# Attention and two gated MLPs on one core: k'v of two heads as two 64x64 products, tokens in five even chunks

## The chip, the core and the metric

The kernel runs on one core of one Trainium2 chip. The metric is the device time of one execution in microseconds (us). A core has a matrix engine (PE, with its weight loads written PEld), a vector engine (DVE), a scalar engine (ACT), GpSimd (POOL) and a queue engine (SP) that issues all DMAs of this kernel; one core's DMAs run on 16 DMA engines.

## What is computed

Three layers in a row, in float32, on 8 batches of 576 tokens with 8 heads of 64 features:

```python
def _attn_ref(q, k, v, g_norm):
    kv = np.einsum('bhsd,bhse->bhde', k, v)          # 64 x 64 for each batch and head
    out = np.einsum('bhsd,bhde->bhse', q, kv)
    rms = np.sqrt(np.mean(out * out, axis=-1, keepdims=True) + 1e-06)
    return out / rms * g_norm

def _moe_ref(x, w_gate, w_val, w_out):               # 4608 x 512, width 1536
    return (1 / (1 + np.exp(-(x @ w_gate))) * (x @ w_val)) @ w_out

def _moe2_ref(x, w_in, w_out):                       # width 2048
    h = x @ w_in
    g = np.where(h >= 1, h, np.where(h <= -1, 0.0, (h + 1) ** 2 / 4))
    return g @ w_out
```

The change is in the first line, the sum over 576 tokens that gives `kv`.

## The kernel before

Tokens go through in nine blocks of 512 (`T`). Two heads make a pair: 128 features, one chunk of x. A large product is three float32r products of halves of its operands (`mm3`, L77 to L79), each of a 128x128 weight tile with 512 columns. The order of instructions on every engine is the order in which the code is written (`tc.manual_schedule()`).

The sum k'v of one batch b and pair p is made by `kv_sum(b, p)` (L109 to L115), 32 times in all. Its tokens lie on the partitions. 576 tokens are four chunks of 128 (`NSC`) and a rest of 64 (`SR`); each chunk is one float32 product of 128 columns of k with 128 columns of v (L113), the rest another with 64 rows (L114), all into one 128x128 tile of PSUM, `kvps`. Only the two 64x64 blocks on its diagonal are k'v of the two heads; `kv_blocks` (L117) copies these into the block-diagonal tile `kvbd`, and `attn_out` (L130) multiplies q with it into `X`. A float32 product is two records of the matrix engine in the trace, so one sum is eight records of L113 and two of L114.

What a sum reads is loaded by SP. For batches 0 and 1, `load_kv_early` (L84) issues a load of k (L88), one of v (L89), 256 KB each on 128 partitions, and one of the rest (L90, 64 partitions, 64 KB); a load of q (256 KB) follows each. SP's order at the start is the four pairs of batch 0 (k, v, rest, q each), `eye`, `spread_f`, two 512 KB loads of weights (L267), the four pairs of batch 1, four more loads of weights. For batches 2 to 7, `load_kv` (L93) loads k and v of a pair in one DMA of 512 KB (L95, tile `kvraw`) and the rest in another (L97). A `kvraw` tile lies in the same ring of four buffers as the raw weights. 

The stages: sums of batch 0 and 1, their norms (`SSt` L171, `rt` L190, `R` L203) and the first gate and value products (`h`, from L77), in one written order up to 52 us; then two blocks through all gate and value products while the weights are decoded from float64 (56 to 193 us; the sums of batch 2 stand here, two at a time, without other work between them); then the down products of these two blocks (193 to 258 us), where blocks of g come back from DRAM (`load_g` L397, DMA at L399, `gload`) and the sums of batch 3 stand; then blocks 2 to 8 one after another, with the sums of batches 4 to 7 beside them, one at a time; from 900 us on the second MLP.

Of the kernel before, what the change touches and what calls it, by code (L numbers as in the profile page):

```python
# [7 lines left out]
F32 = mybir.dt.float32  # L8
# [5 lines left out]
B, H, S, D = 8, 8, 576, 64  # L14
NT, DM, FF1, FF2 = B * S, H * D, 1536, 2048
P = 128
T = 512                 # tokens of a block
NB = NT // T
NP = H // 2             # pairs of heads: one chunk of 128 features each
KC = DM // P  # L20
TC = T // P
F1, F2 = FF1 // P, FF2 // P
NSC = S // P            # whole chunks of 128 tokens of a batch; half a chunk remains
SR = S - NSC * P
NKV = 3                 # batches whose k'v is held
EPS = 1e-6


# [1 line left out]
def attn_gated_mlp_kernel(ctx: ExitStack, tc: tile.TileContext, a: dict, out: bass.AP):  # L30
# [30 lines left out]
        nc.vector.tensor_copy(out=o, in_=i)  # L61

    def split(src, hi, lo):
        """A float32 tile as the exact sum of two tiles of twelve bits each."""
        act_copy(hi, src)
        nc.vector.tensor_tensor(out=lo, in0=src, in1=hi.bitcast(F32), op=ALU.subtract)  # L66
        return hi, lo
# [5 lines left out]
        return tp.tile([P, T], F32, name=name, tag=tag, **kw)  # L73

    def mm3(ps, w, x, first, last, wsl=slice(None)):
        """ps += w.T @ x of float32 operands, as three products of their halves."""
        nc.tensor.matmul(ps, w[0][:, wsl], x[0], start=first, stop=False)  # L77
        nc.tensor.matmul(ps, w[0][:, wsl], x[1], start=False, stop=False)  # L78
        nc.tensor.matmul(ps, w[1][:, wsl], x[0], start=False, stop=last)  # L79

# [1 line left out]
    kvraw, qraw, xnext, state, xs = {}, {}, {}, {}, {}  # L82

    def load_kv_early(b, p):  # L84
        k, v, r = (wp.tile([P, T], F32, name="kv_early", tag="w") for _ in range(3))
        k, v = (x.rearrange("p (c n) -> p c n", c=NSC) for x in (k, v))
        r = r[0:SR, 0:2 * P].rearrange("p (i n) -> p i n", i=2)
        nc.sync.dma_start(out=k, in_=a["kv_main"][b, p][:, 0])  # L88
        nc.sync.dma_start(out=v, in_=a["kv_main"][b, p][:, 1])  # L89
        nc.sync.dma_start(out=r, in_=a["kv_rest"][b, p])  # L90
        kvraw[b, p] = k, v, r

    def load_kv(b, p):  # L93
        t = tp.tile([P, 2, NSC, P], F32, name="kvraw", tag="raw", bufs=4)
        nc.sync.dma_start(out=t, in_=a["kv_main"][b, p])  # L95
        r = tp.tile([SR, 2, P], F32, name="kvrest", tag="rest", bufs=2)
        nc.sync.dma_start(out=r, in_=a["kv_rest"][b, p])  # L97
        kvraw[b, p] = t[:, 0], t[:, 1], r
# [9 lines left out]

    def kv_sum(b, p):  # L109
        k, v, r = kvraw.pop((b, p))  # L110
        ps = at_p.tile([P, P], F32, name="kvps", tag="at")
        for c in range(NSC):
            nc.tensor.matmul(ps, k[:, c, :], v[:, c, :], start=c == 0, stop=False)  # L113
        nc.tensor.matmul(ps, r[:, 0, :], r[:, 1, :], start=False, stop=True)  # L114
        return ps  # L115

    def kv_blocks(b, p, ps, copy):  # L117
        for e in range(2):
            s = slice(e * D, (e + 1) * D)
            copy(kvbd[b % NKV][s, p, s], ps[s, s])  # L120

    def segments(j):
        t = j * T
# [4 lines left out]
            t = e  # L128

    def attn_out(j, p, sqtag="sq", x=None):  # L130
        """q (k'v) of a pair of heads, its product with g_norm and its square."""
        q = qraw.pop((j, p))
        X = at_p.tile([P, T], F32, name="X", tag="at")
        for b, t0, t1 in segments(j):
            nc.tensor.matmul(X[:, t0:t1], kvbd[b % NKV][:, p, :], q[:, t0:t1], start=True, stop=True)  # L135
        if x is None:
            x = xnext[p] = xp.tile([P, T], F32, name="xn", tag=f"xn{p}")
        nc.scalar.activation(out=x, in_=X, func=AF.Copy, scale=gn)
        sq = temp("sq", sqtag)
        nc.scalar.activation(out=sq, in_=X, func=AF.Square)  # L140
        return sq
# [16 lines left out]
        nc.vector.reciprocal(out=r, in_=r)  # L158

    def newton(m, r, t):  # L160
        """r * t is 1 / sqrt(m) to float32's accuracy."""
        nc.scalar.activation(out=t, in_=r, func=AF.Square)
        nc.vector.tensor_tensor(out=t, in0=t, in1=m, op=ALU.mult)
        nc.scalar.activation(out=t, in_=t, func=AF.Copy, scale=-0.5, bias=1.5)

    # while other work is short: the norms of all heads together, tokens on the partitions
    def early_squares(j, p, sq):
        if p == 0:
            state[j] = acc_p.tile([P, TC, H], F32, name="SSt", tag="acc0")
# [33 lines left out]
            nc.tensor.matmul(R, spread[:, p, :], state[j][i], start=i == 0, stop=i == 1)  # L203
        nc.vector.tensor_tensor(out=xnext[p], in0=xnext[p], in1=R, op=ALU.mult)

    # the same with heads on the partitions
    def middle_squares(j, p):
        sq = state.pop((j, p))
        if p == 0:
# [13 lines left out]
        nc.vector.tensor_tensor(out=r, in0=r, in1=t, op=ALU.mult)  # L223
        state[j] = split(r, *(tp.tile([H, T], F32R, name="rt", tag=g) for g in ("sq", "sql")))

    # beside other work: each pair of heads on its own, sums on every partition of its head
    def late_norm(j, p):
        hi, lo = state.pop((j, p))
        SS = at_p.tile([P, T], F32, name="SS", tag="at")
# [11 lines left out]
        nc.vector.tensor_tensor(out=x, in0=x, in1=t, op=ALU.mult)  # L241

    def late_piece(j, n):
        """Step n of 9 that make x of a block, beside other work."""
        p = n // 2
        if n % 2 == 0:
            if p:
                late_scale(j, p - 1)
            if p < NP:
                attn_high(j, p)  # L250
                attn_low(j, p)
                if p + 2 < NP:
                    load_q(j, p + 2)
        else:
            late_norm(j, p)
# [3 lines left out]
            hi, lo = tiles[c] if tiles else (half_tile(xp, f"xh{c}", f"xh{c}"), half_tile(xp, f"xl{c}", f"xl{c}"))  # L259
            xs[c] = split(xnext.pop(c), hi, lo)  # L260

# [1 line left out]
    raws, wgv, wo, wos = {}, {}, {}, {}  # L263

    def load_raw(key, src):
# [2 lines left out]
        raws[key] = raw  # L268

    def decode_steps(keys, outs, place=None):  # L270
        """The float32 nearest to each float64, from its two words."""
        rs = [raws.pop(k) for k in keys]
        low, high = [r[:, :, 0] for r in rs], [r[:, :, 1] for r in rs]
        n = range(len(rs))
        t = [temp("dt", "dt", bufs=2) for _ in n]
        u = [temp("du", "du", bufs=2) for _ in n]
        tu, uu = ([x.bitcast(U32) for x in y] for y in (t, u))
        for i in n:
            nc.scalar.activation(out=t[i], in_=high[i].bitcast(F32), func=AF.Abs, scale=2.0 ** -112)  # L279
        yield  # L280
        for i in n:
            nc.vector.tensor_scalar(out=uu[i], in0=tu[i], scalar1=3, scalar2=None, op0=ALU.logical_shift_left)
            yield
        for i in n:
            nc.vector.tensor_scalar(out=tu[i], in0=tu[i], scalar1=3, scalar2=0x7F800000, op0=ALU.logical_shift_left, op1=ALU.bitwise_and)
            yield
        for i in n:
            nc.vector.scalar_tensor_tensor(out=t[i], in0=low[i], scalar=2.0 ** -52, in1=t[i], op0=ALU.mult, op1=ALU.mult)
            yield
        for i in n:  # L290
            nc.vector.tensor_tensor(out=u[i], in0=u[i], in1=t[i], op=ALU.add)
            yield
        outs += [place(k) for k in keys] if place else t
        ou = [x.bitcast(U32) for x in outs]
        for i in n:
            nc.vector.scalar_tensor_tensor(out=ou[i], in0=high[i], scalar=0x80000000, in1=uu[i], op0=ALU.bitwise_and, op1=ALU.bitwise_or)
            yield

    def run(steps, n=None):
        """The next n steps, or all that remain."""  # L300
        while n != 0 and next(steps, steps) is not steps:
            n = n and n - 1

# [21 lines left out]
                wgv[f, i] = split(t, half_tile(wp, "w", "w"), half_tile(wp, "w", "w"))  # L325

    def decode_gv_steps(f, *parts):
        """The halves (gate and value) of a chunk of weights, step by step."""
        outs = []
        yield from decode_steps([("gv", f, i) for i in parts], outs)  # L330
        for i, t in zip(parts, outs):
            decoded[f, i] = t
# [6 lines left out]
            load_raw(("wo", f), a["w_o1"][f])  # L339

    def decode_wo(*fs):
        """Kept as they are, or left in DRAM while their place is taken."""
        aside = {4: "gl", 5: "gh"}

        def place(key):
            f = key[1]
            if f in aside:
                return gp.tile([P, T], F32, name="wof", tag=aside[f])
            return wp.tile([P, T], F32, name="wo", tag="w")

        ts = []
        yield from decode_steps([("wo", f) for f in fs], ts, place)
        for f, t in zip(fs, ts):
            if f in aside:
                nc.sync.dma_start(out=wod[f], in_=t)
            else:
                wo[f] = t
# [9 lines left out]
    def split_wo(src, f):  # L367
        wos[f] = split(src[f], half_tile(tp, "woh", "woh", bufs=2), half_tile(tp, "wol", "wol", bufs=2))

# [1 line left out]
    gs, gf, acc = {}, {}, {}  # L371

    def gv_sum(f, i, xs, bank=None, between=None):
# [41 lines left out]
            (act_copy if c % 2 else dve_copy)(t, acc[c])  # L415
            nc.sync.dma_start(out=dst(c), in_=t)

# [1 line left out]
    w2, wo2, g2 = {}, {}, {}  # L419

    def load_w2(f):
# [15 lines left out]
        return h  # L437

    def act2(j, f, h):
        # t = clip((h + 1) / 2, 0, 1); the activation is t * max(h, t)  # L440
        t = temp("t2", "sig")
        nc.scalar.activation(out=t, in_=h, func=AF.Relu, bias=half, scale=0.5)  # L442
        g = temp("g2", "gf")
# [17 lines left out]
    def rows(j):  # L461
        return lambda c: out[j * T + c * P:j * T + (c + 1) * P, :]

# [1 line left out]
    todo = [(f, i) for f in range(F2) for i in range(2)]  # L465
    with tc.manual_schedule():
        for p in range(NP):
# [32 lines left out]
        nc.scalar.activation(out=half, in_=half, func=AF.Sqrt)  # L500
        nc.gpsimd.memset(half, 0.5)

        # two blocks through the first products at once, while the weights come in
        def early_attention(j, xs):
            sq = {}
            for n in range(NP + 2):
# [259 lines left out]
```

## Time and profile before

| what | value |
|---|---|
| device time, median of 3 runs | 1824.23 us (1816.62 to 1824.81) |
| profiled execution: span from first to last instruction | 1813.3 us |
| PE busy | 1801.8 us, 99% of the span |
| PE weight loads busy | 1468.4 us, 81% |
| DVE busy | 1056.5 us, 58% |
| ACT busy | 753.6 us, 42% |
| records of the k'v sums on PE | 256 of L113, 64 of L114 |

Of the profiled execution the page gives the span; the device times are longer by what lies ahead of the first instruction and behind the last, 10.9 us at the median. Matmul records overlap each other, so PE's busy share says that it seldom waits, not that each record is as short as it can be: for the time that one takes, read the distance from one start to the next.

### The profile page before, as it was taken

What the parts mean: (1) busy time and instruction counts of PE and PEld (TensorE: products, weight loads), DVE (VectorE), ACT (ScalarE), POOL (GpSimd) and SP (SyncE); (2) the same over time, 40 slices, a digit from 0 to 9 for tenths busy, and PEclk for the clock granted to TensorE, in tenths of its full rate; (3) what the DMA queues carried; (4) which work ended last, traced back from release to release, by engine and by line L of the source; (5) the groups of instructions that cost most, each with busy time, mean ns of one, the idle gap of its engine ahead of it and who ended that gap; (6) DMA issues with size and microseconds to landing.
All of it is one profiled execution on the core that took longest, in us unless ns stands there. A gap on an engine that the chain in (4) does not pass through costs nothing.

```text
span 1813.3 us, 20577 instructions
## 1 busy us (share of the span) xinstructions
PE 1801.8 (99%) x7952; PEld 1468.4 (81%) x7952; DVE 1056.5 (58%) x1621; ACT 753.6 (42%) x1233; POOL 1.8 (0%) x9
## 2 busy tenths in 40 slices
PE   8999999999999999999999999999999999999999
PEld 6787788888888888887888888888888888888887
DVE  3788745756667575775633555454545555555554
ACT  4354344545454454554532434343433333333333
POOL 0000000000000000000000000000000000000000
PEclk9999999999999999999999999999999999999999
DMA  7554623131322322112022201010101010101000
GB/s 222 179 170 161 209 95 104 49 119 67 100 73 66 108 76 78 59 59 76 7 70 82 98 30 47 1 47 1 47 1 47 0 47 0 47 1 47 1 24 24
DMA packets 55954, 124.10 MB, mean 68 GB/s; under 512 B 6568, under 2 KB 8744, under 8 KB 55856
## 3 DMA queue, kind: packets, MB, share of 16 engines
q1 hardware_dynamic: 55856, 122.79, 20.4%
q8 instruction: 62, 1.02, 0.2%
q14 instruction: 36, 0.29, 0.1%
HBM read 88.69 MB, written 34.08 MB: 68 GB/s over the span
## 4 chain that ended last, share of the span: by engine, by line
PE 98%; DVE 1%; DMA 0%; issue 0%; ACT 0%; SPq 0%; DVEq 0%; ACTq 0%
PE h L77 18%; PE h L78 18%; PE h L79 18%; PE acc L77 13%; PE acc L79 13%; PE acc L78 13%; PE X L135 2%; PE kvps L113 2%; PE kvps L114 1%; PE SSt L171 0%; PE R L203 0%; PE SS L230 0%; PE SS L231 0%; DMA gload<-gd 0%; DMA kv_early<-in_kv_main 0%
## 5 line engine op out<-in xcount | busy, mean ns | idle before, releaser
L77 PE MATMUL h<-xh,w 128*128 128x512 f32 x1344 | 527.3, 392 | 0.0
L78 PE MATMUL h<-xl,w 128*128 128x512 f32 x1344 | 525.5, 391 | 0.0
L79 PE MATMUL h<-xh,w 128*128 128x512 f32 x1344 | 524.7, 390 | 0.2 <-DVE w L66 0.2
L77 PEld LDWEIGHTS h<-xh,w 128*128 128x128 f32 x1344 | 252.8, 188 | 56.4 <-ACT dt L279 0.4
L79 PEld LDWEIGHTS h<-xh,w 128*128 128x128 f32 x1344 | 252.7, 188 | 55.3 <-DVE w L66 0.6
L78 PEld LDWEIGHTS h<-xl,w 128*128 128x128 f32 x1344 | 252.7, 188 | 54.0
L444 DVE SCALAR_TENSOR_TENSOR g<-t,h 128x512 f32<-128x512 f32 x144 | 98.9, 687 | 249.9 <-ACT t L442 248.8
L442 ACT ACTIVATE t<-h,half 128x512 f32<-128x512 f32 x144 | 99.2, 689 | 261.0 <-PE h L79 261.0
L388 DVE TENSOR_TENSOR gf<-sig,h 128x512 f32<-128x512 f32 x108 | 74.0, 685 | 194.1 <-PE h L79 102.9
L66 DVE TENSOR_TENSOR wol<-wo,woh 128x512 fp32r<-128x512 f32 x252 | 172.5, 685 | 15.4 <-ACT woh L58 15.4
L77 PE MATMUL acc<-gh,woh 128*128 128x512 f32 x432 | 177.2, 410 | 0.0
L79 PE MATMUL acc<-gh,wol 128*128 128x512 f32 x432 | 171.2, 396 | 0.1
L78 PE MATMUL acc<-gl,woh 128*128 128x512 f32 x432 | 171.0, 396 | 0.0
L58 ACT ACTIVATE woh<-wo 128x512 fp32r<-128x512 f32 x252 | 155.5, 617 | 14.2 <-PE acc L79 13.5
L77 PE MATMUL acc<-woh,gh 128*128 128x512 f32 x384 | 150.5, 392 | 0.0
L79 PE MATMUL acc<-woh,gl 128*128 128x512 f32 x384 | 150.2, 391 | 0.0
L78 PE MATMUL acc<-wol,gh 128*128 128x512 f32 x384 | 149.4, 389 | 0.0
L58 ACT ACTIVATE gh<-gf 128x512 fp32r<-128x512 f32 x84 | 53.0, 631 | 212.8 <-DVE gf L388 212.8
L58 ACT ACTIVATE gh<-g 128x512 fp32r<-128x512 f32 x96 | 60.7, 632 | 143.4 <-DVE g L445 143.4
L386 ACT ACTIVATE sig<-h 128x512 f32<-128x512 f32 x108 | 64.6, 598 | 115.4 <-PE h L79 107.6
L66 DVE TENSOR_TENSOR gl<-g,gh 128x512 fp32r<-128x512 f32 x96 | 66.5, 693 | 67.0 <-ACT gh L58 67.0
L445 DVE SCALAR_TENSOR_TENSOR g<-t,g 128x512 f32<-128x512 f32 x144 | 99.5, 691 | 5.0
(127 smaller groups left out, 2143.2 us busy)
## 6 DMA issues: line engine op xcount, KB each, us to landing
raw<-in_w SPq DMA_DIRECT2D x32, 512.0 KB, 3.8
raw<-in_w_gv SPq DMA_DIRECT2D x24, 512.0 KB, 4.7
kvraw<-in_kv_main SPq DMA_DIRECT2D x24, 512.0 KB, 5.0
x2d<-ev SPq DMA_DIRECT2D x36, 256.0 KB, 2.7
xn<-x2d SPq DMA_DIRECT2D x36, 256.0 KB, 4.5
out<-ev SPq DMA_DIRECT2D x36, 256.0 KB, 4.1
w2d<-dt SPq DMA_DIRECT2D x32, 256.0 KB, 2.4
qraw<-in_qT SPq DMA_DIRECT2D x28, 256.0 KB, 3.5
```

The source lines that it names most:

```text
L58: nc.scalar.activation(out=o, in_=i, func=AF.Copy)
L66: nc.vector.tensor_tensor(out=lo, in0=src, in1=hi.bitcast(F32), op=ALU.subtract)
L77: nc.tensor.matmul(ps, w[0][:, wsl], x[0], start=first, stop=False)
L78: nc.tensor.matmul(ps, w[0][:, wsl], x[1], start=False, stop=False)
L79: nc.tensor.matmul(ps, w[1][:, wsl], x[0], start=False, stop=last)
L113: nc.tensor.matmul(ps, k[:, c, :], v[:, c, :], start=c == 0, stop=False)
L135: nc.tensor.matmul(X[:, t0:t1], kvbd[b % NKV][:, p, :], q[:, t0:t1], start=True, stop=True)
L386: nc.scalar.activation(out=sig, in_=gate, func=AF.Sigmoid)
L388: nc.vector.tensor_tensor(out=g, in0=sig, in1=value, op=ALU.mult)
L442: nc.scalar.activation(out=t, in_=h, func=AF.Relu, bias=half, scale=0.5)
L444: nc.vector.scalar_tensor_tensor(out=g, in0=t, scalar=1.0, in1=h, op0=ALU.min, op1=ALU.max)
L445: nc.vector.scalar_tensor_tensor(out=g, in0=t, scalar=1.0, in1=g, op0=ALU.min, op1=ALU.mult)
```

## The change

Tokens are cut into five chunks: four of 116 (`SC`) and one of 112 (`SR`). The loads carry 116 and 112 partitions in place of 128 and 64; a partition of a main load still holds the same 2 KB (4 KB in `load_kv`), one of the rest 1 KB. For each chunk, two products are made in place of one: the columns 0 to 63 of k with columns 0 to 63 of v into partitions 0 to 63 of `kvps`, and columns 64 to 127 with columns 64 to 127 into partitions 64 to 127. `kvps` is 128x64. No product has 64 rows any more. The host cuts the arrays accordingly; comments are gone. Line numbers from `kv_sum` on are higher by up to three.

```diff
+SC = 116
-SR = S - NSC * P
+SR = S - NSC * SC
     def load_kv_early(b, p):
         k, v, r = (wp.tile([P, T], F32, name="kv_early", tag="w") for _ in range(3))
-        k, v = (x.rearrange("p (c n) -> p c n", c=NSC) for x in (k, v))
+        k, v = (x[0:SC].rearrange("p (c n) -> p c n", c=NSC) for x in (k, v))
     def load_kv(b, p):
-        t = tp.tile([P, 2, NSC, P], F32, name="kvraw", tag="raw", bufs=4)
+        t = tp.tile([SC, 2, NSC, P], F32, name="kvraw", tag="raw", bufs=4)
     def kv_sum(b, p):
         k, v, r = kvraw.pop((b, p))
-        ps = at_p.tile([P, P], F32, name="kvps", tag="at")
-        for c in range(NSC):
-            nc.tensor.matmul(ps, k[:, c, :], v[:, c, :], start=c == 0, stop=False)
-        nc.tensor.matmul(ps, r[:, 0, :], r[:, 1, :], start=False, stop=True)
+        ps = at_p.tile([P, D], F32, name="kvps", tag="at")
+        chunks = [(k[:, c], v[:, c]) for c in range(NSC)] + [(r[:, 0], r[:, 1])]
+        for c, (kc, vc) in enumerate(chunks):
+            for e in range(2):
+                s = slice(e * D, (e + 1) * D)
+                nc.tensor.matmul(ps[s], kc[:, s], vc[:, s], start=c == 0, stop=c == NSC)
     def kv_blocks(b, p, ps, copy):
-            copy(kvbd[b % NKV][s, p, s], ps[s, s])
+            copy(kvbd[b % NKV][s, p, s], ps[s])
```

On PE, the last two early sums (batch 1, pairs 2 and 3) and the first product of the MLP stand like this before (`kvps` is k'v, `SSt` the sums of squares, `h` the first gate product):

```order
L113 MATMUL kvps<-kv_early 128x128 x4
L114 MATMUL kvps<-kv_early 128x128
L171 MATMUL SSt<-ones_136,sq 128x2 x4
L135 MATMUL X<-q_early,kvbd_139 128x64
L135 MATMUL X<-q_early,kvbd_140 128x448
L113 MATMUL kvps<-kv_early 128x128 x4
L114 MATMUL kvps<-kv_early 128x128
L171 MATMUL SSt<-ones_136,sq 128x2 x4
L77 MATMUL h_469<-xh_431,w 128x512
```

and like this after:

```order
L117 MATMUL kvps<-kv_early 64x64 x10
L174 MATMUL SSt<-ones_136,sq 128x2 x4
L138 MATMUL X<-q_early,kvbd_139 128x64
L138 MATMUL X<-q_early,kvbd_140 128x448
L117 MATMUL kvps<-kv_early 64x64 x10
L174 MATMUL SSt<-ones_136,sq 128x2 x4
L78 MATMUL h_509<-xh_466,w 128x512
```

Nothing moved: ten products stand where five stood, and both sums still stand ahead of the first h.

On SP, the loads for the sums of batch 3 and the loads of g among them stand like this before:

```order
L95 DMA kvraw<-in_kv_main 128x1024
L97 DMA kvrest<-in_kv_rest 64x256
L95 DMA kvraw<-in_kv_main 128x1024
L97 DMA kvrest<-in_kv_rest 64x256
L399 DMA gload<-gd_8_107 128x512
```

and like this after:

```order
L96 DMA kvraw<-in_kv_main 116x1024
L98 DMA kvrest<-in_kv_rest 112x256
L96 DMA kvraw<-in_kv_main 116x1024
L98 DMA kvrest<-in_kv_rest 112x256
L402 DMA gload<-gd_8_107 128x512
```

The order is the same; the shapes of the loads differ.

## Rows read from the trace of the kernel before

**Rows 1.** The page: busy time by engine, and the last chain by engine

```profile
PE 1801.8 (99%) x7952; PEld 1468.4 (81%) x7952; DVE 1056.5 (58%) x1621; ACT 753.6 (42%) x1233; POOL 1.8 (0%) x9
...
PE 98%; DVE 1%; DMA 0%; issue 0%; ACT 0%; SPq 0%; DVEq 0%; ACTq 0%
```

**Rows 2.** Stages: length, busy by engine (records), granted clock, DMA share, GB/s

```profile
4.20:22.00 17.80, 16.15 (x77) 12.24 (x78) 0.42 (x1) 7.13 (x18) 0.00 (x0) 1.00 0.95 299
22.00:29.00 7.00, 7.00 (x27) 5.07 (x28) 3.79 (x11) 2.14 (x7) 0.00 (x0) 0.52 1.07 309
200.00:228.00 28.00, 27.90 (x126) 21.98 (x125) 21.50 (x40) 11.25 (x20) 0.00 (x0) 1.00 0.61 205
```

**Rows 3.** PE in order of time, a sum of batch 4: start, length, line, tile

```profile
287.92 0.39 PE L231 MATMUL SS<-sql,ones 128*128 128x512 f32 x1
288.15 1.05 PE L113 MATMUL kvps<-kvraw 128*128 128x128 f32 x8
289.14 0.48 PE L114 MATMUL kvps<-kvrest 64*128 64x128 f32 x2
289.55 0.50 PE L77 MATMUL acc<-gh,woh 128*128 128x512 f32 x1
289.89 0.40 PE L78 MATMUL acc<-gl,woh 128*128 128x512 f32 x1
```

**Rows 4.** PE in order of time, small products of the early stage

```profile
18.09 1.05 PE L171 MATMUL SSt<-ones,sq 128*128 128x2 f32 x8
19.00 1.10 PE L135 MATMUL X<-q_early,kvbd 128*128 128x512 f32 x2
19.94 0.28 PE L171 MATMUL SSt<-ones,sq 128*128 128x2 f32 x2
...
47.36 0.39 PE L79 MATMUL h<-xh,w 128*128 128x512 f32 x1
47.67 1.04 PE L190 MATMUL rt<-eye,early_r 128*8 128x128 f32 x8
```

**Rows 5.** PE in order of time, last early sum and first h

```profile
36.88 1.05 PE L113 MATMUL kvps<-kv_early 128*128 128x128 f32 x8
37.86 0.48 PE L114 MATMUL kvps<-kv_early 64*128 64x128 f32 x2
38.28 1.05 PE L171 MATMUL SSt<-ones,sq 128*128 128x2 f32 x8
39.19 0.48 PE L77 MATMUL h<-xh,w 128*128 128x512 f32 x1
```

**Rows 6.** DMA: 0 to 3.6 us in 40 slices; issues, KB, us to landing

```profile
GB/s 0 0 0 0 0 0 0 0 0 0 0 0 0 0 0 0 0 0 0 23 0 23 228 341 296 319 387 387 387 364 410 410 364 387 387 410 376 217 159 114
...
kvraw<-in_kv_main SPq DMA_DIRECT2D x24, 512.0 KB, 5.0
...
kv_early<-in_kv_main SPq DMA_DIRECT2D x16, 256.0 KB, 5.4
...
spread_f<-in_spread SPq DMA_DIRECT2D x1, 16.0 KB
```

**Rows 7.** SP in order of time, three loads of kvraw: start, length

```profile
196.55 0.33 SPq L95 DMA_DIRECT2D kvraw<-in_kv_main  x1
...
210.37 0.33 SPq L95 DMA_DIRECT2D kvraw<-in_kv_main  x1
...
275.14 0.55 SPq L95 DMA_DIRECT2D kvraw<-in_kv_main  x1
```

**Rows 8.** DMA: the loads issued at 196.55 and 210.37, us to landing

```profile
kvraw<-in_kv_main SPq DMA_DIRECT2D x1, 512.0 KB, 4.3
...
kvraw<-in_kv_main SPq DMA_DIRECT2D x1, 512.0 KB, 3.9
```

**Rows 9.** PE in order of time, where two sums of batch 3 start

```profile
202.21 0.49 PE L113 MATMUL kvps<-kvraw 128*128 128x128 f32 x3
...
215.02 0.27 PE L113 MATMUL kvps<-kvraw 128*128 128x128 f32 x1
```

**Rows 10.** The last chain, 212 to 223 us: start, us, what

```profile
212.55 4.76 DMA gload<-gd
217.42 0.64 ACT gh L58
...
223.05 0.50 PE acc L79
```

More of the change, by code (lines that the diff above doesn't have):

```diff
@@ L736 @@
     kv = np.stack([pairs(k), pairs(v)], axis=2)
-    main = kv[:, :, :, :NSC * P].reshape(B, NP, 2, NSC, P, P).transpose(0, 1, 4, 2, 3, 5)
-    rest = kv[:, :, :, NSC * P:].transpose(0, 1, 3, 2, 4)
+    main = kv[:, :, :, :NSC * SC].reshape(B, NP, 2, NSC, SC, P).transpose(0, 1, 4, 2, 3, 5)
+    rest = kv[:, :, :, NSC * SC:].transpose(0, 1, 3, 2, 4)
     def cols(w):
```

## Prediction

> **What bounds the kernel now.** I read the page's busy times and its last chain first: PE is busy for 99% of the span and carries 98% of the chain [rows 1]. So two things cost time: PE's own work, and whatever makes PE wait. The table of stages comes next. In the first 22 us the DMA engines are full (share 0.95, 299 GB/s), as they are to 29 us [rows 2]: PE computes there what has just come in. At 200 to 228 us PE has 0.1 us of idle time in 28, but the chain runs through a load of g [rows 2, 10]. Everywhere else the DMAs are light and PE alone sets the pace. The change touches both kinds: the products of the sums, and the shape of the loads that feed them.
>
> **The products.** A sum of batch 4 shows the price. From the first record of the sum to the second product behind it 1.74 us pass (288.15 to 289.89), 0.23 of which the first product would have taken anyway (the spacing 287.92 to 288.15): a sum costs 1.51 us [rows 3]. Eight records of 128 rows take 0.99 us, 0.11 of spacing at the end of a chain of weight loads included. The two records of 64 rows take 0.41: two streams of 0.107, one weight load of 0.107 that nothing hides, and some 0.09 that the engine drains before it takes another tile shape [rows 3]. The same happens on the way out.
>
> After, a sum is 20 records of 64 weight columns and 64 moving columns. Two rows say what each half costs. Eight products with 2 moving columns take 0.91 us, 0.114 each: that is the load of 128 weight columns. Two with 512 float32 columns take 0.94, 0.117 for each 128 columns: that is the stream [rows 4]. Half of either is 0.056. The way into a tile of fewer columns is in rows 4 as well: the product at 47.36 is followed by one of 8 weight columns after 0.31 us, in place of 0.23. So one sum should cost 0.31 (drain) + 0.055 (first load) + 19 x 0.056 = 1.06 + 0.15 (last stream and drain) + 0.107 (load of 128 columns) - 0.23 = 1.45 us, 0.06 less than now. Batches 2 to 7 hold 24 sums that PE pays in full: -1.4 us. The four of batch 2 stand in twos, which saves two changes of shape of 0.35: **-2.1 us** together. No row shows 64-column products, so I bound them. If both halves of the array worked side by side, a record would cost 0.028: 19 x 0.028 less, -0.53 more a sum, **-14 us** in all. If a 64-column load cost as much as one of 128, a record would be 0.112 and a sum 2.62: **+27 us**. I take 0.056, since loads and streams in rows 4 both go by the column.
>
> **The loads.** A main load keeps its bytes per partition and loses 12 partitions. What matters is on how many of the 16 DMA engines it runs. All loads of the kernel before have 128 or 64 partitions, equal shares for 16 engines, except one: `spread_f` with 8 rows, the one issue whose row has no time to landing [rows 6], as if fewer than 16 engines reported. 116 partitions are not 16 equal shares; the largest number up to 16 that divides them is 4 (29 each). 112 gives 16 shares of 7. The bounds are 4 engines and 16; I take 4, by the odd row.
>
> The Trainium skill says just this in "DMA: Bandwidth & Descriptors", section "Why a DMA increments its semaphore by 16 and not by 1": on a queue like SP's, a DMA uses the largest number of engines up to 16 that divides the partition count, and the sequencer posts the missing completions itself (its examples: 100 partitions give 10 engines, 127 give 1). By that rule 116 gives 4; by 16 equal engines the loads would cost what they do now. The missing landing of an 8-row load agrees with it; no run so far shows 116.
>
> Alone on the line, the first loads move 364 to 410 GB/s, 390 at the middle, over 16 engines: 24.4 GB/s each [rows 6]. A load of k or v (116 x 2 KB = 237,568 bytes) on four engines takes 237,568 / 97.5 GB/s = 2.44 us instead of 262,144 / 390 = 0.67. A `kvraw` (475,136 bytes) takes 4.87 instead of 1.34: 3.5 us more. Everything that shares these four engines queues behind it.
>
> **Early stage.** The last early sum stands ahead of the first h on PE, and starts at 36.88 us; h follows at 39.19 [rows 5]. In SP's order, 16 loads of k and v are done when it can start: 16 x 2.44 = 39.0 us on the four engines. With them go 8 rests (0.29 each, 2.3), 7 loads of q (0.67 each, 4.7) and two of weights (1.34 each, 2.7): 48.8 us. First bytes move at 1.8 us [rows 6] and a load is known about 1 us after its last byte, so 51.6 at best; at the 299 GB/s of the full stage [rows 2] the same work ends at 66. I take 54, near the best, since twelve engines idle most of that time. That is +17.1 on 36.88. PE is then mostly idle between sums, and the row of 22 to 29 us shows the granted clock at 0.52, the lower of its two levels (1.2 GHz), in a stage with gaps ahead of it [rows 2]: the last sum and the products of squares (1.4 and 0.9 us now, [rows 5]) would take twice as long, +2.3. Early stage: **+19.4**, bounds 14.7 and 31. The eight early sums themselves cost nothing more: they stand beside these waits. The weight loads that follow come 20 us later too, but so do their users.
>
> **Batch 2** (70 to 87 us): the loads have some slack, and the second of two queues behind the first; raw weights queue behind both. **+1**, bounds 0 and 4.
>
> **Batch 3.** The load for its first sum goes out at 196.55 and lands 4.3 us later, at 200.85; the sum starts at 202.21 [rows 7 to 9]. With 3.5 more it lands at 204.35: PE waits 2.1. The second goes out at 210.37, lands after 3.9, and its sum starts at 215.02: 0.75 of slack against 3.5 [rows 7 to 9]. Worse, a second `kvraw` and then the load of g at 212.55 stand behind it on the queue. That load of g is on the chain: 4.76 us, then ACT, DVE, and PE at 223.05 [rows 10]. Behind two longer loads it lands 7.0 later, and the 2.75 that the sum waits lies within these 7. Stage: 2.1 + 7.0 = **+9.1**, bounds 2 and 10.
>
> **Batches 4 to 7.** Block 4's first load goes out at 275.14 and its sum starts at 288.15 [rows 3, 7]: 13 us for 5.0 + 3.5. Hidden, as are the others, which follow at a sum's distance (some 19 us) or more.
>
> **The sum** is made on the profiled execution, a span of 1813.3 us; the median of the runs, 1824.2, is 10.9 above it, outside the instructions and untouched. -2.1 + 19.4 + 1 + 9.1 = +27.4, so 1824.2 + 27.4 = 1851.6, about **1852 us**.
>
> **Rivals.** (a) *Sixteen engines.* If a load of 116 partitions is spread over all 16 DMA engines (8 rows on the fullest), no load gets longer, every wait above vanishes and the products alone remain: 1824.2 - 2.1 = **1822**. For it: nothing in the trace shows 4 engines. Against it: the odd row of `spread_f`. The point from which it decides: a load of k or v under 1.5 us, that is on more than six engines, since 51.6 - 16 x (2.44 - 1.5) is where the last early sum starts now.
>
> (b) *The halves run side by side.* Two products on different columns need not wait for each other: 1852 - 14 = **1838**. Against it: rows 4 show a load of 128 columns to be a stage of its own that takes all of 0.11, one at a time.
> The Trainium skill gives ground for (b) in "TensorEngine Tiling (Array Packing)", section "Key Properties": tiles work independently, loads and products of different tiles can go in parallel, and only a change of the mode drains the engine. By it the products would be 14 us cheaper than now; no row shows two tiles at work.
>
> (c) *Half a load costs a whole one:* 1852 + 29 = **1881**. For it: no row has 64 columns. Against it: eight products with 8 weight columns (`rt`) take 1.04 us with the last one's tail, 0.11 each, the stream alone [rows 4]: a load of few columns is short enough to hide.
>
> **Chances.** The forecast 0.60, (a) 0.16, (b) 0.13, (c) 0.11. The range reaches from (b) less its uncertainty to the early bound of 31 with the batch 3 stage: 1830 to 1874; (a) and most of (c) lie outside. 0.5% is 9 us, about what a measurement of this kernel can tell from no change: slower by more takes the forecast, (b), (c) and a little of (a) (with costlier products): 0.84; within, most of (a): 0.12; faster, (a) with (b): 0.04.
>
> **What would show it.** The time to landing of `kv_early` and `kvraw`: 5.4 and 5.0 us now, over 8 in the forecast, unchanged in (a). The start of the first h: 39.2 now, 57 to 60 in the forecast. The DMA rate while k and v come in: near 100 to 150 GB/s against 299. PE waiting for `kvraw` at about 220 to 250 us, and for none from batch 4 on. A sum in batch 4: 20 records in 1.06 us, 0.056 apart; 0.028 in (b), 0.112 in (c). It is wrong if the loads land as now, or if the first h starts late and the end does not.

## The result, and the profile after

| | median of the runs | ratio to before, 95% interval |
|---|---|---|
| before | 1820.42 us (4 runs beside the changed kernel, 1815.96 to 1824.81) | |
| after | 1848.85 us (4 runs, 1846.16 to 1850.88) | 1.0142 [1.0106, 1.0178] |

The kernel became slower by 28.4 us, or 19 to 32 by the interval of the ratio. The profiled execution after took 1848.39 us, with a span of 1846.6: only 1.8 us lie outside the span. From span to span it lost 1846.6 - 1813.3 = 33.3 us. The two differences part because the profiled execution before was a quick one (1813.3 + 1.8 = 1815.1 us, against a median of 1820.42).

The page of the changed kernel, busy time by engine and the last chain by engine, against [rows 1]:

```profile
PE 1805.4 (98%) x8272; PEld 1462.9 (79%) x8272; DVE 1057.4 (57%) x1621; ACT 753.2 (41%) x1233; POOL 1.9 (0%) x9
...
PE 93%; DMA 5%; DVE 1%; issue 0%; SPq 0%; ACT 0%; DVEq 0%; ACTq 0%
```

PE has all but the same work; the chain has gone from 0% DMA to 5%. What PE waits for stands in the groups of instructions (busy, mean ns | idle time before them, and what ended it):

```profile
L117 PE MATMUL kvps<-kvraw 116*64 116x64 f32 x384 | 17.2, 235 | 13.5 <-DMA kvraw<-in_kv_main 13.5
...
L117 PE MATMUL kvps<-kv_early 116*64 116x64 f32 (+1 forms) x160 | 10.7, 318 | 19.1 <-DMA kv_early<-in_kv_main 19.1
```

**Where it went.** I paired each PE record that both traces have with its partner, and read how much later it starts. The table gives the places where this delay changes.

| the same record | before, us | after, us | delay |
|---|---|---|---|
| start of the last early sum | 36.88 | 58.11 | 21.2 |
| first product of h | 39.19 | 61.10 | 21.9 |
| last product ahead of batch 2 | 56.81 | 81.65 | 24.8 |
| products behind the first two sums of batch 2 | 73.08 | 96.44 | 23.4 |
| products behind the other two sums of batch 2 | 88.94 | 118.51 | 29.6 |
| products ahead of the third sum of batch 3 | 221.42 | 265.68 | 44.3 |
| product behind the last sum | 678.37 | 711.73 | 33.4 |

The delay rises in three places, to 44.3 us. From there it falls by 0.57 us with each of the last 18 sums, and less than 1 us of it comes back in any other way. So the change has two sides, as forecast, but both are larger than forecast: the late loads, with the lower clock that comes with them, cost about 48 us, and the products give back about 14.

**The products.** PE in order of time, a sum of batch 4 (against [rows 3]):

```profile
330.46 0.40 PE L234 MATMUL SS<-sql,ones 128*128 128x512 f32 x1
330.78 0.69 PE L117 MATMUL kvps<-kvraw 116*64 116x64 f32 x16
331.30 0.29 PE L117 MATMUL kvps<-kvrest 112*64 112x64 f32 x4
331.51 0.50 PE L78 MATMUL acc<-gh,woh 128*128 128x512 f32 x1
331.85 0.40 PE L79 MATMUL acc<-gl,woh 128*128 128x512 f32 x1
```

From the first record of the sum to the product behind it 0.73 us pass, where [rows 3] show 1.40. The way in costs more (0.32 in place of 0.23, since even the first record now has another tile shape), the way out as much as before (0.34). Twenty records start within 0.58 us. The starts of six of them, read one by one, tell how (start in us; by their order in the code, the heads):

```
330.948   first head
330.954   second head
331.006   first head
331.013   second head
331.064   first head
331.071   second head
```

The two heads of a chunk start 0.007 us apart and the next pair 0.058 after the last. They run side by side on PE's two column halves; e5 below tests that.

**The early loads.** The DMA engines from 4.2 to 40 us in 40 slices, and the issues with their time to landing (against [rows 2, 6]):

```profile
GB/s 324 97 104 133 274 181 98 94 148 214 208 92 98 94 101 114 204 295 104 96 144 302 279 270 256 77 97 101 205 207 206 108 96 98 204 272 96 94 98 187
...
kv_early<-in_kv_main SPq DMA_DIRECT2D x10, 232.0 KB
...
kv_early<-in_kv_rest SPq DMA_DIRECT2D x6, 112.0 KB, 11.7
```

Whenever loads of k and v are alone on the line, the rate stands at 92 to 104 GB/s, a quarter of the 390 of [rows 6]: four DMA engines. The main loads have lost their landing time, like `spread_f` in [rows 6]. The rests behind them land after 11.7 us. PE at the end of the stage, in order of time (against [rows 5]):

```profile
58.11 1.33 PE L117 MATMUL kvps<-kv_early 116*64 116x64 f32 x20 [2.03 <-DMA kv_early<-in_kv_main]
59.37 1.87 PE L174 MATMUL SSt<-ones,sq 128*128 128x2 f32 x8
61.10 0.77 PE L78 MATMUL h<-xh,w 128*128 128x512 f32 x1
...
62.10 0.63 PE L80 MATMUL h<-xh,w 128*128 128x512 f32 x1
62.53 0.63 PE L78 MATMUL h<-xh,w 128*128 128x512 f32 x1
```

The last sum waits for its load. The products of squares behind it take 1.87 us where [rows 5] have 1.05, and products of h start 0.43 us apart (62.10 to 62.53) where [rows 3] have 0.23: PE runs at the lower of its two clock levels, 1.2 GHz, as it has done in all the sums so far (the last section).

**Batches 2 and 3.** What PE waited for from 61 to 270 us (us in total, times, longest); before, no wait for a `kvraw` stood there:

```profile
PE kvps L117 <- DMA kvraw<-in_kv_main: 13.5, 4, 4.9
```

SP's issues in batch 3, and PE's sums and the product that waits for the load of g (against [rows 7, 9]):

```profile
226.28 0.28 SPq L96 DMA_DIRECT2D kvraw<-in_kv_main  x1
...
227.50 0.38 SPq L402 DMA_DIRECT2D gload<-gd  x1
...
245.47 0.28 SPq L96 DMA_DIRECT2D kvraw<-in_kv_main  x1
...
246.18 0.32 SPq L96 DMA_DIRECT2D kvraw<-in_kv_main  x1
...
247.03 3.16 SPq L402 DMA_DIRECT2D gload<-gd  x3
```

```profile
237.04 1.12 PE L117 MATMUL kvps<-kvraw 116*64 116x64 f32 x16 [4.94 <-DMA kvraw<-in_kv_main]
...
254.52 0.69 PE L117 MATMUL kvps<-kvraw 116*64 116x64 f32 x16 [3.27 <-DMA kvraw<-in_kv_main]
...
261.87 0.63 PE L78 MATMUL acc<-gh,woh 128*128 128x512 f32 x1 [2.03 <-ACT woh L59]
```

The first sum's load goes out at 226.28 and the sum starts at 237.04: 10.8 us, where the load alone took 4.3 in [rows 8]. The second pair is 245.47 and 254.52, 9.0 us against 3.9. The load of g behind two `kvraw` takes the place that it had in [rows 10], with 13.53 us instead of 4.76 (the chain that ended last):

```profile
247.03 13.53 DMA gload<-gd
...
260.67 0.63 ACT gh L59
261.30 0.53 ACT woh L59
...
261.87 0.63 PE acc L78
```

From batch 4 on PE waits for no load of k or v, as forecast.

### The profile page after: what moved, and what is told of

The parts are those of the page before. It is cut to its first block, busy times and chain, and to the rows that moved or that the text cites. A ratio compares the mean times of both kernels' runs of the same rounds, so it can differ in the third digit from the quotient of the medians.

```text
span 1846.6 us, 21195 instructions
## 1 busy us (share of the span) xinstructions
PE 1805.4 (98%) x8272; PEld 1462.9 (79%) x8272; DVE 1057.4 (57%) x1621; ACT 753.2 (41%) x1233; POOL 1.9 (0%) x9
## 4 chain that ended last, share of the span: by engine, by line
PE 93%; DMA 5%; DVE 1%; issue 0%; SPq 0%; ACT 0%; DVEq 0%; ACTq 0%
PE h L78 17%; PE h L79 17%; PE h L80 17%; PE acc L78 12%; PE acc L80 12%; PE acc L79 12%; DMA kv_early<-in_kv_main 2%; PE X L138 1%; DMA gload<-gd 1%; PE kvps L117 1%; DMA q_early<-in_qT 1%; DMA kvraw<-in_kv_main 1%; PE SS L234 0%; PE SS L233 0%; PE R L206 0%
## 5 line engine op out<-in xcount | busy, mean ns | idle before, releaser
L59 ACT ACTIVATE woh<-wo 128x512 fp32r<-128x512 f32 x252 | 155.5, 617 | 13.5 <-PE acc L80 13.5
```

Source lines behind the costliest of these rows:

```text
L59: nc.scalar.activation(out=o, in_=i, func=AF.Copy)
```

## Experiments

Two theories were to be told apart. The first: the loss comes from loads of 116 partitions that run on four DMA engines, and the halves are a gain. The rival: the halves or the uneven cut of the tokens, as such, cost something beside the loads. Each edit below is against the changed kernel or the experiment named. Ratios are to runs of the kernel before on the same chip.

**e1: chunks of 112 and a rest of 128, two halves.** Both partition counts are multiples of 16; all else is the changed kernel.

```
-SC = 116
+SC = 112
```

> The changed kernel with chunks of 112, 112, 112, 112 and 128 tokens in place of 116 (four times) and 112: the same two 64x64 products per chunk, loads of 112 and 128 partitions. Theory A (the loss is in the loads: 116 partitions travel on few DMA engines, 112 = 16 x 7 on all; the products are cheaper): the loads land as in the kernel before (kvraw near 5 us, first h near 36 to 39 us, no wait for kvraw), a sum costs 0.93 us as in the changed kernel against 1.51, so 24 sums give 0.57 x 24 = 14 us and the early stage some 2 more: 1804 us, 1798 to 1810, faster than the kernel before. Theory B (the loss is in uneven cuts as such, any row count but 128 and 64): loads slow as with 116 rows, near 1849. Theory C (the two-column products disturb something else early): the first h stays near 60 us.

Measured: 1808.84 us, ratio 0.9933 [0.9909, 0.9957]. The changed kernel took 1848.85: four partitions less in a load make some 40 us. No wait for a `kvraw` is left, and a sum takes the same 0.73 us. It came out nearly 5 us over the expected 1804. Against the kernel before, its PE records are 7.0 us late at 64 us, and a sum then gains 0.57. Something early costs time although the loads are short again; e9 and e10 look at that.

**e2: the same cut, one product of 128x128 per chunk.**

```
-SC = 116
+SC = 112
...
-            for e in range(2):
-                s = slice(e * D, (e + 1) * D)
-                nc.tensor.matmul(ps[s], kc[:, s], vc[:, s], start=c == 0, stop=c == NSC)
+            nc.tensor.matmul(ps, kc, vc, start=c == 0, stop=c == NSC)
```

The tile `kvps` and the copies out of it are those of the kernel before.

> Chunks of 112 (four) and 128 tokens, but one 128x128 product per chunk as in the kernel before: only the cut is changed, and with it the product of 64 rows is gone. Theory A: ten records 0.112 apart without a change of tile shape, 1.12 us a sum against 1.51 before and 0.93 with two halves: 0.39 x 24 = 9 us less than before, 1811 us, 1806 to 1816, some 5 us above the version with halves. If halves as such made the whole gain, it would stay at the kernel before, 1820.

Measured: 1805.91 us, ratio 0.9933 [0.9908, 0.9959], at the lower edge of the expected. A sum of batch 3, PE in order of time:

```profile
227.65 1.05 PE L115 MATMUL kvps<-kvraw 112*128 112x128 f32 x8
228.54 0.39 PE L115 MATMUL kvps<-kvrest 128*128 128x128 f32 x2
228.69 0.48 PE L78 MATMUL acc<-gh,woh 128*128 128x512 f32 x1
```

The sum takes 1.04 us (227.65 to 228.69) instead of 1.40. The even cut alone, without the change of tile shape that the 64-row rest had, gives 0.39 us from one sum to the next. The halves give 0.19 more. And yet e1 and e2 take the same time.

**e3: the loads of the changed kernel (116 and 112), products of 128x128.** The edit of e2 without the change of `SC`.

> The loads of the changed kernel (116 and 112 partitions) with one 128x128 product per chunk: the products are undone, the loads kept. Theory A: the same waits for loads as in the changed kernel (first h near 61 us, waits at batches 2 and 3), and sums of 1.12 us in place of 0.93 for the 18 to 20 sums that wait for nothing: 1849 + 4 = 1853 us, 1849 to 1857. Theory C (the products of two halves make the loss): back to 1810 to 1820.

Measured: 1853.27 us, ratio 1.0199 [1.0162, 1.0235], as expected. The waits come with the loads, whatever the products are:

```profile
PE kvps L115 <- DMA kvraw<-in_kv_main: 10.8, 3, 4.5
```

Its delay against the kernel before is 44.6 us at 267 us, like that of the changed kernel (44.3), and then falls by 0.39 a sum.

**e4: 112 partitions for batches 0 and 1 alone, 116 for the rest, two halves.** The early loads read from arrays of their own, cut at 112.

```
+SCE = 112
+SRE = S - NSC * SCE
...
-        k, v = (x[0:SC].rearrange("p (c n) -> p c n", c=NSC) for x in (k, v))
+        k, v = (x[0:SCE].rearrange("p (c n) -> p c n", c=NSC) for x in (k, v))
```

> Chunks of 112 and 128 tokens for batches 0 and 1, of 116 and 112 for batches 2 to 7; two halves throughout: the early loads alone are put right. Theory A, with costs that add: the early stage's 25 us go, the waits at batch 2 (6 us) and batch 3 (15 us) stay: 1849 - 25 = 1824 us, 1818 to 1830, or 20 us above the version with 112 throughout. If a late early stage is what makes the later waits (everything shifted against the loads), they go too and it ends near 1804.

Measured: 1829.66 us, ratio 1.0039 [1.0003, 1.0074], at the upper end of the expected. The delay ahead of batch 2 is 4.7 us in place of 24.8, so 20 us of the loss belong to the early loads. The waits of batches 2 and 3 stay: 13.7 us for `kvraw` in three waits, against 13.5 in four, and the delay grows to 26.3 us at the end of batch 3's waits, by 21.6 where the changed kernel has 19.4. So these waits don't come from the late early stage.

**e5: e1 with all five chunks of the first head first.** No two neighbours lie on different columns, except at the change of head.

```
-        for c, (kc, vc) in enumerate(chunks):
-            for e in range(2):
-                s = slice(e * D, (e + 1) * D)
+        for e in range(2):
+            s = slice(e * D, (e + 1) * D)
+            for c, (kc, vc) in enumerate(chunks):
```

> The kernel of e1 (112 and 128 tokens a chunk, two halves) with the twenty records of a sum in another order: five chunks of the first head, then five of the second, so that no two neighbours lie on different columns of PE. Theory 'side by side' (the pairs of the changed kernel start 0.007 us apart and 0.058 from pair to pair because neighbours use different columns): without neighbours on other columns the records stand about 0.056 apart, a sum of ten products takes about 0.29 to 0.56 us more, 24 sums give +7 to +13 us and the early sums some more: 1816 to 1823 us. Rival 'a record of 64 columns costs 0.029 wherever it stands': 1809 us as e1, with the same 0.73 us from the first record to the next product.

Measured: 1812.56 us, ratio 0.9951 [0.9931, 0.9972]. The interval overlaps that of e1, so the time doesn't decide; the sum does. PE in order of time, batch 3:

```profile
229.60 0.73 PE L117 MATMUL kvps<-kvraw 112*64 112x64 f32 x10
230.11 0.22 PE L117 MATMUL kvps<-kvrest 128*64 128x64 f32 x1
230.17 0.22 PE L117 MATMUL kvps<-kvraw 112*64 112x64 f32 x1
...
230.52 0.28 PE L117 MATMUL kvps<-kvrest 128*64 128x64 f32 x2
230.73 0.51 PE L78 MATMUL acc<-gh,woh 128*128 128x512 f32 x1
```

1.13 us from 229.60 to 230.73, against 0.73 in e1, and 0.06 from record to record (230.11 to 230.17). The gain hangs on neighbours that lie on different columns. 24 x 0.40 = 9.6 us were to be lost over e1 and 3.7 show: the profiled execution of e5 reached batch 2 earlier than that of e1 (74.2 against 77.3 us), so the early stage hid part of it.

**e6: chunks of 120 and a rest of 96, two halves** (the edit of e1 with 120).

> Loads of 120 partitions (four chunks of 120 tokens and a rest of 96), two halves as in e1. Theory 'the largest number up to 16 that divides the partitions' (the Trainium skill, DMA: Bandwidth & Descriptors): 15 engines, a load hardly longer than at 112 partitions, 1805 to 1815 us. Rival 'the greatest common divisor with 16' (which also makes 4 of 116): 8 engines, loads of twice the length, a third of what 4 engines cost, 1819 to 1826 us. Rival 'what matters is an uneven cut as such': 1845 to 1853 us as in the changed kernel.

Measured: 1812.22 us, ratio 0.9944 [0.9922, 0.9966]. The interval overlaps that of e1: an uneven cut as such costs nothing that these runs show. 120 is no multiple of 16 and the loads land in time; in the whole profile, issues with KB and us to landing:

```profile
kvraw<-in_kv_main SPq DMA_DIRECT2D x24, 480.0 KB, 6.1
```

6.1 us against 5.5 with 112 partitions in e1, and nothing like the 9 to 11 of the changed kernel. Eight engines would have made a load alone 1.3 us longer, which this number doesn't exclude by itself. The first loads do, while k and v are alone on the line (to 2.9 us; 0 to 4.2 us in 40 slices, against [rows 6]):

```profile
GB/s 0 0 0 0 0 0 0 0 0 0 0 0 0 0 0 0 98 156 137 156 254 390 410 351 332 410 390 312 283 312 263 224 176 176 176 146 215 156 244 273
```

They move at up to 410 GB/s, as in the kernel before, where eight engines at 24.4 would stop at 195. So the rival of eight engines falls. Fifteen fit, and the rate doesn't tell them from 16.

**e7: chunks of 118 and a rest of 104, two halves** (the edit of e1 with 118).

> Loads of 118 partitions (four chunks of 118 tokens and a rest of 104), two halves. Theory 'as many engines as divide the partitions': 2 engines, a load of k or v lasts 4.9 us instead of 2.4, a whole main load 9.8; the first h starts near 110 us, and the batch 3 waits grow to some 5 us for each of the four loads: 1910 to 1950 us. Rival 'anything that isn't a multiple of 16 costs about the same': 1845 to 1855 us.

Measured: 1918.51 us, ratio 1.0537 [1.049, 1.0583]. The DMA engines from 4.2 to 110 us, and what PE waited for in the whole span:

```profile
GB/s 135 49 48 48 167 49 49 49 134 83 48 49 152 184 290 46 57 50 167 50 50 81 125 57 49 48 119 97 50 48 91 292 283 279 85 53 29 0 3 3
```

```profile
PE kvps L117 <- DMA kv_early<-in_kv_main: 56.5, 8, 13.0
PE kvps L117 <- DMA kvraw<-in_kv_main: 36.6, 6, 9.2
```

The rate with k and v alone is 48 to 50 GB/s, half of that at 116 partitions: two engines. Two partitions more cost 70 us. The Trainium skill's rule ("DMA: Bandwidth & Descriptors", section "Why a DMA increments its semaphore by 16 and not by 1": the largest number of engines up to 16 that divides the partitions) gives 4, 2, 15 and 16 for 116, 118, 120 and 112; the four kernels order themselves so, the rates at 116 and 118 agree with it, and the rate at 120 excludes eight.

**e8: the halves alone**, with the chunks of 128 and the rest of 64 of the kernel before (the edit of e1 with 128).

> The halves alone: the chunks stay at 128 tokens and a rest of 64, as in the kernel before, so that no load changes, and each product is cut into two heads. Theory 'neighbours on other columns run side by side': eight records of 128 rows in four pairs 0.058 us apart, then one change of shape for the two records of 64 rows (some 0.2 us in the kernel before), so 0.6 to 0.75 us from the first record to the next product where the kernel before takes 1.40, less 0.19 for the way in and out; a gain of 0.45 to 0.6 us for each of 24 sums, 1804 to 1811 us. Rival 'the gain of the halves hangs on the even cut': no gain over before, 1816 to 1822 us.

Measured: 1806.56 us, ratio 0.9916 [0.9889, 0.9944]. PE in order of time, a sum of batch 3:

```profile
232.12 0.69 PE L117 MATMUL kvps<-kvraw 128*64 128x64 f32 x16
232.74 0.33 PE L117 MATMUL kvps<-kvrest 64*64 64x64 f32 x4
233.00 0.50 PE L78 MATMUL acc<-gh,woh 128*128 128x512 f32 x1
```

0.88 us a sum, more than the 0.6 to 0.75 expected, but the time is in the range: the two halves need no even cut. What 64 rows cost is smaller here than with whole products, 0.15 over e1's 0.73, so the gains of the cut (0.39) and of the halves (0.43 in this kernel) don't add up; both together give 0.57. Although no load changed, its records are 5.1 us late ahead of batch 2, in one execution of each: an early loss as in e1, with the loads of the kernel before.

**e9 and e10: the two mixes.** Chunks of 112 and a rest of 128. In e9 the sums of batches 0 and 1 are one product per chunk and the others two halves; in e10 it is the other way round (`b > 1`).

```
+        whole = b < 2
+        ps = at_p.tile([P, P if whole else D], F32, name="kvps", tag="at")
...
+            if whole:
+                nc.tensor.matmul(ps, kc, vc, start=c == 0, stop=c == NSC)
+                continue
...
```

> 112 and 128 tokens a chunk; the sums of batches 0 and 1 as one product of 128x128 per chunk, those of batches 2 to 7 as two halves. Theory: in e1 the halves made the sums of the early stage no cheaper, as PE waits for loads there, and the granted clock stood at its lower level longer (0.50 to 0.65 from 36 to 48 us, where e2 shows 0.92 to 1.00). So this kernel keeps the early stage of e2 and the later sums of e1 (18.75 us from sum to sum instead of 18.94): 24 x 0.19 = 4.5 us under e2, 1801 us (1797 to 1805). Rival 'the halves had no part in the early clock, which varies from execution to execution': as e1 with its own scatter, 1804 to 1810 us.

> The other mix of e1 and e2: halves in batches 0 and 1, one product of 128x128 per chunk in batches 2 to 7, chunks of 112 and 128 tokens. Theory 'the halves of the early stage cost time, by a clock that stays at its lower level longer': e1 stands 8.5 us over the mix e9, which differs in the early sums alone, so this kernel stands as far over e2 (1805.9): 1811 to 1816 us, with the last early sum at 38 to 42 us and the granted clock under 0.7 for most of 36 to 48 us. Rival 'the early stage scatters from execution to execution, whatever the form of its sums': 1804 to 1808 us, with the same early times as e2.

Measured: e9 1800.27 us, ratio 0.9898 [0.987, 0.9925], the fastest of all kernels here; e10 1814.78 us, ratio 0.9953 [0.9929, 0.9977], beside runs in which the kernel before took 1824.25. Both medians fell into the ranges of the theory of the clock; but beside e2 the kernel before took 1818.79, so about 5 of the 9 us between e10 and e2 are not the kernel's. The end of the early stage in e9, and then in e10, PE in order of time:

```profile
33.51 1.28 PE L117 MATMUL kvps<-kv_early 112*128 112x128 f32 x10
34.62 0.95 PE L178 MATMUL SSt<-ones,sq 128*128 128x2 f32 x8
35.43 0.48 PE L78 MATMUL h<-xh,w 128*128 128x512 f32 x1
```

```profile
41.82 1.34 PE L121 MATMUL kvps<-kv_early 112*64 112x64 f32 x20
43.08 1.87 PE L178 MATMUL SSt<-ones,sq 128*128 128x2 f32 x8
44.81 0.77 PE L78 MATMUL h<-xh,w 128*128 128x512 f32 x1
```

The same eight products of squares take 0.95 and 1.87 us, and h starts 9.4 us later in e10. The granted clock of e10 was 0.50 from 36 to 48 us, that of e9 1.00. Over all kernels whose loads are short, the early sums that ran at the full level, out of eight in the one profiled execution of each, are (by the spacing of their records):

| form of the early sums | kernel: sums at the full level |
|---|---|
| one product of 128x128 | before 5, e2 3, e9 5 |
| halves | e1 1, e4 0, e5 2, e6 1, e8 0, e10 0 |

No kernel with halves has as many as any kernel without. That the halves keep the clock down is thus likely and not shown: what in them would do it wasn't tried, and it isn't the same in all executions: of the 12 of e10 three took 1805.6 to 1805.8 us and nine 1811.9 to 1818.0. The price is therefore known roughly. e1 less e9 is 0.9933 - 0.9898, or 6 us, e10 less e2 is 0.9953 - 0.9933, or 4 us, and the intervals of both pairs overlap.

## Why the prediction was right, and where it was not

The forecast was 1852 us, +27.4; measured were 1848.85, +28.4. The direction and the cause stood: loads on four DMA engines, early stage first, then batch 3, batches 4 to 7 hidden. e1, e3, e4, e6 and e7 show this cause: with 112 or 120 partitions the loss is gone, with 118 it grows, and it comes with the loads whatever the products. But that +27.4 lies within 1 us of +28.4 is luck: the loads were put at 29.5 us and cost about 48, the products at -2.1 and gave about -14, and the profiled execution that the sum started from was a quick one.

**Products: -2.1 forecast, about -14 found.** The step that failed is "I take 0.056". Rival (b) was right in its mechanism: 0.058 for a pair, 0.029 a record. Its own term, -14 us, is what the delay shows: 20 sums x 0.57, and 1.5 for each of the two double sums of batch 2, 14.4. I had argued against it from a load of 128 columns that takes 0.11 as a stage of its own [rows 4]. That row is about one tile after another, and says nothing of two tiles at once; e5 has just that spacing, 0.06, when neighbours share their columns. The Trainium skill's sentence in "TensorEngine Tiling (Array Packing)", section "Key Properties", that loads and products of different tiles go in parallel, deserved more than 0.13: the trace agrees, with 0.007 us between the two records. The time that I gave (b), 1838, counts the -2.1 twice: with -14 in its place the sum is 1840.

**Early stage: +19.4 forecast, 24.8 found.** Four engines at 97.5 GB/s were right (92 to 104). The last load was taken to be there at 54 and its sum started at 58.11: "I take 54, near the best" was too hopeful, since the loads of q and the weights stand between those of k and v, and SP issues the last `kv_early` only at 43.51. The chain that ended last:

```profile
17.65 11.66 DMA q_early<-in_qT
...
30.10 13.40 DMA kv_early<-in_kv_main
...
43.51 14.46 DMA kv_early<-in_kv_main
```

Each link is a load that must land before its room, or the work behind it, lets SP issue the next. The clock had its own error. Up to the first h I had put it at +2.3, and it came to 0.7 (2.99 us from the start of the sum to h, against 2.31), as the halves make the sum shorter. The forecast ended there, at a delay of 21.9; but the spacing stays at the lower level until 64 us, which brings 23.3, and a second stretch with a granted clock of 0.50, from 74.4 to 81.1 us, brings 24.8. Kernels whose early loads are short are late at this place as well, by 1.0 to 9.0 us with halves (e6 the least, e10 the most) and 1.7 in e2, not at all in e9. With the long loads the form of the products makes little difference: e3 has 26.1.

**Batch 2: +1 forecast, about 7.7 found** (29.6 - 24.8, and the 3.0 that the products had gained by then). The slack that I named was worked out for one load that grows by 3.5 us. Here two `kvraw` share four engines, and land 11.1 and 11.5 us after their issue, against 5.0 in the median [rows 6]. PE in order of time:

```profile
108.02 0.69 PE L117 MATMUL kvps<-kvraw 116*64 116x64 f32 x16 [0.41 <-DMA kvraw<-in_kv_main]
...
113.67 1.12 PE L117 MATMUL kvps<-kvraw 116*64 116x64 f32 x16 [4.85 <-DMA kvraw<-in_kv_main]
```

The second wait is 4.85 us, and the records behind it start at the lower clock level (1.12 us for the sixteen instead of 0.69).

**Batch 3: +9.1 forecast, about 16 found** (44.3 - 29.6, and the 1.1 that two sums had gained). The place was right to the load: first sum, second sum, load of g. The size was made of 3.5 us a load, worked out for a load alone; the first `kvraw` landed some 10.8 us after its issue, 6.5 more than before. Two more sources of delay were not in the sum: PE comes out of such a wait at its lower clock level, as the 1.12 us of the sixteen records at 237.04 shows, and the load of g took 8.8 us longer where I had 7.0. What else holds a single `kvraw` for 11 us I did not separate; other loads and a write of g share its four engines in that stretch.

**The base.** "10.9 above it, outside the instructions and untouched" was wrong, and so is the sentence on the 10.9 us under the table of the kernel before. In every run on record 1.7 to 1.9 us lie outside the span; the rest is the difference between a quick execution that was profiled and the median. Taken from span to span, the forecast of +27.4 stands against 33.3.

**Rival (a)** fell with the rate of 92 to 104 GB/s, **rival (c)** with the sum of 0.73 us. Of the marks that I had named, the landing, the rate, the waits for `kvraw` in batch 3 (they end at 237 and 254.5 us) and the quiet batches 4 to 7 came as forecast. The waits in batch 2 were not among them; the first h, 57 to 60, came at 61.10; and the 20 records of a sum stand 0.029 apart, the mark of (b).

## What to carry to other kernels

Cut a tensor's rows so that the partitions of each load are a multiple of 16, or at least have a large divisor up to 16 (120 was as good as 112 here): 112 in place of 116 is worth some 40 us, and what makes the products even can leave the loads a quarter of the engines. Two block-diagonal products of 64 columns that stand next to each other run side by side at half the spacing of the whole product (0.058 us for a pair, 0.11 for a record of 128x128). After the changes of tile shape 0.19 us a sum is left of that (e1 against e2), so they pay where PE sets the pace; where PE waits for loads anyway, as in the early stage, they save nothing and seem to cost clock. Price a load on few engines by its queue: not by its own added bytes, but by all that stands ahead of it and behind it on those engines.

## What the runs showed of the hardware

**The granted clock goes with the scatter.** In 16 runs of the kernel before, beside e1 to e4, the mean granted clock and the time go together: 0.997 with 1814.5 to 1817.3 us, 0.995 with 1818.5 to 1820.7, 0.989 to 0.992 with 1824.5 to 1829.8. The profiled execution before was of the first sort, and the stretches at the lower level that its trace records end by 56 us. Where they lie in the slower runs is not shown, as these left no trace. So one profile of a kernel can stand 4 to 9 us under the median of its runs without any time outside the span.

**The column of the granted clock starts with its first record.** The trace of the changed kernel holds no record of the granted clock before 64.1 us (that of the kernel before, none before 11.7), and the view counts a stretch without a record as 1.00. Two stretches, the first without a record (length, busy by engine, granted clock, DMA share, GB/s; the second is of PE alone):

```profile
4.20:22.00 17.80, 7.34 (x54) 3.94 (x56) 0.00 (x0) 3.22 (x8) 0.00 (x0) 1.00 0.50 154
...
112.00:118.00 6.00, 4.33 (x27) 0.50 0.75 266
```

All eight early sums took 1.02 us from their first record to their last, at any place, and so did the sum at 113.67, where the column says 0.50; the sum at 330.78 takes 0.58. So PE was at its lower level in all the early sums, although the column has 1.00 for them. Ahead of the first record it is the spacing of the matmul records that tells the level; behind it, column and spacing agree in the stretches that are shown here.
